# The first head drawn into TensorE's loop, and two small weights loaded ahead of the first keys, in a cached-attention decode kernel

## The chip, the cores and the metric

One core of one Trainium2 chip. The metric is device time of one execution in microseconds (us), as a median over runs. A profile's span ends some 2 us before the time, so spans are compared with spans and times with times.

## The reference, cut to what matters

```python
# x: 1 x 512; 32 heads, 65536 cached keys of 128 (bf16): K and V are 537 MB each
q = (x @ wq)                                   # 512 x 4096
scores = einsum("bhqd,bhkd->bhqk", q, k_cache) * Dh ** -0.5
o = einsum("bhqk,bhkd->bhqd", softmax(scores), v_cache)
a = o @ wo
b = (silu(x @ w_gate) * (x @ w_up)) @ w_down   # 512 x 1792, 1792 x 512
g = sigmoid((x * gate_w).sum())
return g * a + (1 - g) * b
```

Every byte of K and V is read once and used once: 1088 MB in all, with few operations for each byte.

## The kernel before

K and V pass through a ring of three slots in SBUF (the core's on-chip memory), 8.4 MB each. A head is two chunks; a chunk is one K load and one V load. VectorE multiplies K in place by q, TensorE sums the products with the identity as weights (`block`), VectorE and ScalarE finish the exponentials (`gather`), and TensorE forms P·V (`pv`). A slot is loaded again once its last reader has finished. The start shares slot 0 between wq, gate and up:

```python
dma("wq", wq_sb, ..., units(0, 0, WQ))                     # slot 0
...
load("k", 0, [EK] * (KPP // EK))                           # slot 1, four pieces
dma("gate", gate_v, ..., units(0, G0, U0))                 # slot 0
dma("up", up_v, ..., units(0, U0, U0 + KT * F))            # slot 0
load("v", 0, [KPP])                                        # slot 2
...
spread(0)                                  # q of head 0 to all partitions
for n in range(N - 1):                     # chunks, two to a head
    h, c = divmod(n, CH)
    if c == 0:
        cut[h] = len(plan.ops)
    if n:
        load("k", n, [KPP])                # the third load of the ring onwards
        load("v", n, [KPP])
    m = EK if n in (0, N - 2) else HK
    for j in range(0, KPP, m):
        ...
        block(n, j, m)
        ...
        while len(todo) > 1:
            gather()
    gather()
    if n == 0:
        gate()                             # sigmoid gate
        hidden()                           # 112 products with gate and up: frees slot 0
    ...
    pv(n)
```

All operations are recorded first and then emitted. TensorE's are emitted as straight code for head 0, a hardware loop of ten rounds of three heads (1 to 30), and straight code for head 31:

```python
first, last = 1, 1 + rounds * BODY         # BODY = 3, rounds = 10
for o in pe(0, cut[first]):
    put(o, o.waits)
...
with nc.Fori(0, rounds, 1, engines=[PE], head_slot={PE: 0}) as r:
    for i, o in enumerate(body[0]):
        put(o, {s: val + r * step[i, s] for s, val in o.waits.items()})
for o in pe(last, len(plan.ops)):
    put(o, o.waits)
```

`head_slot={PE: 0}` asks for the loop's first instruction at the start of an instruction-fetch block. TensorE's code is fetched in blocks of 16 KB, the packets of queue q8 below (13 of 16,384 bytes in the kernel before). The built program of that kernel holds 3483 entries for TensorE (instructions and 7 labels) in 222,912 bytes, 64 bytes each, so a packet holds 256.

The softmax here doesn't subtract the row's maximum and nothing guards it: scores larger than these inputs give would overflow.

## Time and profile before

| | before |
|---|---|
| median time | 2518.3 us |
| bytes moved by DMA | 1088 MB |
| mean DMA rate over the span | 432 GB/s |
| TensorE, VectorE busy | 78%, 50% |
| second K load issued; data queued before it lasts until | 52.0 us; 61.8 us |
| last V piece used by TensorE from; span | 2512.1 us; 2516.7 us |

From the page of the kernel before: the DMA row in 40 slices of the span (9 is 90% or more busy), the rate in each slice, and two of the DMA queues with packets, MB and share of 16 engines.

```profile
DMA  9999999999999999999999999999999999999998
GB/s 423 432 433 433 433 432 437 434 435 434 433 433 433 434 437 433 434 433 433 433 433 434 434 432 435 435 435 435 434 433 433 433 434 436 434 433 434 433 434 376
...
q1 hardware_dynamic: 20744, 1087.78, 99.8%
q8 instruction: 13, 0.21, 0.0%
```

The rate is flat from end to end, except for the first and last slices. The mean over the span is 432 GB/s, with most slices at 433 to 435, and the packets of q1 take 99.8% of the 16 engines' span: by that count the DMA engines are busy from end to end. (Single slices read up to 437, and windows of 78 us up to 440. The view seems to book a packet whole in one window, as 1 us windows of this run read 131 and 918 GB/s; so only means over long stretches are compared.) The page of the kernel before counts 1087.77 MB read from HBM, the chip's main memory, at 432 GB/s. So the time here is bytes over rate, plus what stands outside the stream at both ends. That no kernel could stream faster isn't shown. Queue q8 is taken as TensorE's instruction fetches: 13 packets, 0.21 MB, 16 KB each, beside 0.22 MB of TensorE code in the built program.

The chain of work that ended last tells another story at first sight. Its line by engine:

```profile
DMA 46%; PE 40%; DVE 13%; ACT 1%; issue 0%; another core or an unknown queue 0%; SPq 0%; DVEq 0%; ACTq 0%
```

It goes through TensorE and VectorE for half the span, because each load was released by them. But a load that is issued while others are still queued does not start at its issue (the second K load below is issued at 52.0 us and lands 29 us later, where its 8.4 MB take 19.3), and the chain books the queueing as "DMA". What counts is whether the queue was ever empty. That is read from the issue times. From the timeline of the kernel before, the issuing queue's loads of the start (start us, us of issuing, source):

```profile
1.03 0.38 SPq L181 DMA_DIRECT2D slot_65<-in_A_wq_dram  x1
1.47 1.96 SPq L181 DMA_DIRECT2D slot_66<-in_A_k_cache_dram  x4
3.47 0.44 SPq L181 DMA_DIRECT2D slot_65<-in_B_w_gate_dram  x1
...
4.46 0.48 SPq L181 DMA_DIRECT2D slot_67<-in_A_v_cache_dram  x1
51.99 0.33 SPq L181 DMA_DIRECT2D slot_65<-in_A_k_cache_dram  x1
52.37 0.43 SPq L181 DMA_DIRECT2D slot_66<-in_A_v_cache_dram  x1
```

And the first uses of V0 (TensorE) and of the second K load (VectorE) in the same timeline; the bracket says how long the engine had been idle and for what:

```profile
61.77 16.18 PE L257 MATMUL O_ps<-slot_67,P_sb_83 128*4 128x512 bf16 x64 [9.80 <-DMA slot_67<-in_A_v_cache_dram]
...
81.06 17.29 DVE L344 TENSOR_TENSOR slot_65<-slot_65,q_bc_78 128x16384 bf16<-128x16384 bf16 x2 [27.71 <-DMA slot_65<-in_A_k_cache_dram]
```

The second K load (slot 65) is issued at 52.0 us while V0 is still arriving until 61.8: 9.8 us of cushion. It lands at 81.06, 19.3 us after V0, which is what 8.4 MB take at 434 GB/s. VectorE's 27.7 us of idle time there cost nothing.

The tail of the kernel before, TensorE's timeline, shows two kinds of gap:

```profile
2460.93 6.10 PEld L257 LDWEIGHTS m_c<-P_sb_83,slot_65 128*128 128x128 bf16 x230 [3.16 <-issue]
2461.14 5.95 PE L257 MATMUL m_c<-P_sb_83,slot_65 128*128 128x1 bf16 x229
...
2469.42 0.86 PE L257 MATMUL m_c<-P_sb_83,slot_65 128*128 128x1 bf16 x27 [2.33 <-issue]
...
2502.09 3.44 PE L257 MATMUL m_c<-P_sb_84,slot_65 128*128 128x1 bf16 x127 [1.20 <-ACT P_sb_84 L294]
2508.09 0.18 PE L257 MATMUL m_c<-P_sb_84,slot_65 128*128 128x1 bf16 x1 [2.56 <-issue]
...
2512.12 0.77 PE L257 MATMUL m_c<-P_sb_84,slot_65 128*128 128x1 bf16 x16 [0.43 <-DMA slot_65<-in_A_v_cache_dram]
```

In the columns of P·V of the last head (a column is the 256 products that one chunk's P·V takes here), TensorE loads 128 x 128 weights at about 27 ns each. It stops twice for 2.3 and 2.6 us with no visible wait ("issue"), after 229 products of the first column and after 127 of the last. Then it waits 0.43 us for the last V piece, which ends the kernel.

### The profile page before, as it was taken

The page shows a single profiled execution, that of the slowest core. Times are in us where ns is not written, and L with a number is a line of the kernel's source. Part 1 is how long each engine was busy: PE and PEld are TensorE (multiplying, and loading weights), DVE is VectorE, ACT ScalarE, POOL GpSimd, SP SyncE. Part 2 cuts the span into 40 slices and gives each one's busy share as a digit, 9 for nine tenths or more (in the row PEclk, how much of TensorE's full clock was granted, in tenths as well). Part 3 has the DMA queues.
Part 4 walks back from the last instruction along what each step waited for, and adds up shares of the span by engine and source line. Part 5 has one row for each costly group of instructions (what it writes and reads, how often), then busy time and mean ns, then how long its engine had stood idle before and what let it go on. Part 6 is the DMA issues. An engine that isn't in the chain of part 4 may idle for free.

```text
span 2516.7 us, 15579 instructions
## 1 busy us (share of the span) xinstructions
PE 1972.7 (78%) x9177; PEld 410.3 (16%) x5215; DVE 1268.4 (50%) x291; ACT 99.2 (4%) x404; POOL 1.9 (0%) x9
## 2 busy tenths in 40 slices
PE   4777877877878778778787787787877877877787
PEld 1111111111111111111111111111111111111113
DVE  3455355464553554644545546446455364464554
ACT  0000000000000000000000000000000000000000
POOL 0000000000000000000000000000000000000000
PEclk8899989989889889899898899898988989989898
DMA  9999999999999999999999999999999999999998
GB/s 423 432 433 433 433 432 437 434 435 434 433 433 433 434 437 433 434 433 433 433 433 434 434 432 435 435 435 435 434 433 433 433 434 436 434 433 434 433 434 376
DMA packets 20767, 1088.04 MB, mean 432 GB/s; under 512 B 2314, under 2 KB 2444, under 8 KB 2700
## 3 DMA queue, kind: packets, MB, share of 16 engines
q1 hardware_dynamic: 20744, 1087.78, 99.8%
q8 instruction: 13, 0.21, 0.0%
q14 instruction: 6, 0.05, 0.0%
q10 hardware_dynamic: 4, 0.00, 0.0%
HBM read 1087.77 MB, written 0.00 MB: 432 GB/s over the span
## 4 chain that ended last, share of the span: by engine, by line
DMA 46%; PE 40%; DVE 13%; ACT 1%; issue 0%; another core or an unknown queue 0%; SPq 0%; DVEq 0%; ACTq 0%
PE O_ps L257 17%; DMA slot_67<-in_A_k_cache_dram 16%; DMA slot_65<-in_A_k_cache_dram 14%; DMA slot_66<-in_A_k_cache_dram 14%; PE S_ps_103 L275 11%; PE S_ps_104 L275 8%; DVE slot_66 L344 4%; DVE slot_67 L344 4%; DVE slot_65 L344 3%; DMA slot_65<-in_A_v_cache_dram 2%; DVE S_sb_82 L369 2%; PE m_c L257 1%; PE S_ps_103 L285 1%; ACT P_sb_83 L294 0%; DMA slot_65<-in_A_wq_dram 0%
## 5 line engine op out<-in xcount | busy, mean ns | idle before, releaser
L344 DVE TENSOR_TENSOR slot_67<-slot_67,q_bc_79 128x16384 bf16<-128x16384 bf16 (+1 forms) x28 | 208.2, 7469 | 146.5 <-DMA slot_67<-in_A_k_cache_dram 146.5
L369 DVE TENSOR_REDUCE S_sb_82<-S_ps_104 128x128 f32<-128x1024 f32 (+1 forms) x67 | 78.8, 1177 | 392.0 <-PE S_ps_104 L275 392.0
L344 DVE TENSOR_TENSOR slot_65<-slot_65,q_bc_78 128x16384 bf16<-128x16384 bf16 x22 | 190.2, 8689 | 146.3 <-DMA slot_65<-in_A_k_cache_dram 146.3
L344 DVE TENSOR_TENSOR slot_66<-slot_66,q_bc_78 128x16384 bf16<-128x16384 bf16 (+1 forms) x24 | 190.6, 7978 | 138.0 <-DMA slot_66<-in_A_k_cache_dram 122.5
L344 DVE TENSOR_TENSOR slot_66<-slot_66,q_bc_79 128x16384 bf16<-128x16384 bf16 x20 | 172.9, 8689 | 122.4 <-DMA slot_66<-in_A_k_cache_dram 122.4
L344 DVE TENSOR_TENSOR slot_65<-slot_65,q_bc_79 128x16384 bf16<-128x16384 bf16 x20 | 172.9, 8689 | 120.2 <-DMA slot_65<-in_A_k_cache_dram 120.2
L344 DVE TENSOR_TENSOR slot_67<-slot_67,q_bc_78 128x16384 bf16<-128x16384 bf16 x20 | 172.9, 8689 | 117.8 <-DMA slot_67<-in_A_k_cache_dram 117.8
L275 PE MATMUL S_ps_103<-slot_65,ident 128*128 128x512 bf16 x651 | 186.6, 457 | 0.0
L275 PE MATMUL S_ps_103<-slot_67,ident 128*128 128x512 bf16 x680 | 185.8, 441 | 0.0
L275 PE MATMUL S_ps_103<-slot_66,ident 128*128 128x512 bf16 x650 | 184.9, 454 | 0.0
L257 PE MATMUL O_ps<-slot_67,P_sb_83 128*4 128x512 bf16 x704 | 155.9, 383 | 28.1 <-ACT P_sb_83 L294 18.3
L257 PE MATMUL O_ps<-slot_66,P_sb_84 128*4 128x512 bf16 x704 | 153.7, 379 | 19.3 <-ACT P_sb_84 L294 19.3
L257 PE MATMUL O_ps<-slot_65,P_sb_83 128*4 128x512 bf16 x640 | 139.7, 379 | 18.3 <-ACT P_sb_83 L294 18.3
L257 PE MATMUL O_ps<-slot_67,P_sb_84 128*4 128x512 bf16 x640 | 139.7, 379 | 18.3 <-ACT P_sb_84 L294 18.3
L257 PE MATMUL O_ps<-slot_65,P_sb_84 128*4 128x512 bf16 x640 | 139.7, 379 | 18.3 <-ACT P_sb_84 L294 18.3
L257 PE MATMUL O_ps<-slot_66,P_sb_83 128*4 128x512 bf16 x640 | 139.8, 379 | 17.5 <-ACT P_sb_83 L294 17.5
L275 PE MATMUL S_ps_104<-slot_67,ident 128*128 128x512 bf16 x680 | 150.7, 379 | 0.0
L275 PE MATMUL S_ps_104<-slot_65,ident 128*128 128x512 bf16 x651 | 143.9, 379 | 0.0
L275 PE MATMUL S_ps_104<-slot_66,ident 128*128 128x512 bf16 x650 | 143.9, 379 | 0.0
L285 PE MATMUL S_ps_103<-slot_65,ident 128*128 128x512 bf16 x21 | 12.8, 608 | 134.9 <-DVE slot_65 L344 134.9
L285 PE MATMUL S_ps_103<-slot_66,ident 128*128 128x512 bf16 x22 | 13.2, 598 | 134.2 <-DVE slot_66 L344 134.2
L285 PE MATMUL S_ps_103<-slot_67,ident 128*128 128x512 bf16 x24 | 13.9, 581 | 125.0 <-DVE slot_67 L344 125.0
(99 smaller groups left out, 719.0 us busy)
## 6 DMA issues: line engine op xcount, KB each, us to landing
slot_66<-in_A_k_cache_dram SPq DMA_DIRECT2D x4, 2048.0 KB, 24.4
slot_67<-in_A_k_cache_dram SPq DMA_DIRECT2D x4, 2048.0 KB, 30.7
slot_65<-in_A_wq_dram SPq DMA_DIRECT2D x1, 4096.0 KB, 12.1
slot_66<-in_A_wo_dram SPq DMA_DIRECT2D x1, 4096.0 KB, 32.5
slot_65<-in_A_v_cache_dram SPq DMA_DIRECT2D x1, 4096.0 KB, 37.4
slot_65<-in_A_v_cache_dram SPq DMA_DIRECT2D x1, 2048.0 KB, 40.7
slot_65<-in_B_w_gate_dram SPq DMA_DIRECT2D x1, 1792.0 KB, 34.6
slot_65<-in_B_w_up_dram SPq DMA_DIRECT2D x1, 1792.0 KB, 38.3
```

Of the source, the lines that this page charges most:

```text
L257: ins = nc.tensor.matmul(out_ap, lhsT=a, rhs=b, start=start and i == 0, stop=stop and i == len(pairs) - 1,)
L275: ins = nc.tensor.add_instruction(mybir.InstMatmult(name=nc.get_next_instruction_name(), engine=mybir.EngineType.PE, ins=[nc.tensor.lower_ ...
L285: ins = nc.tensor.matmul(out_ap, lhsT=a, rhs=b, start=first, stop=last)
L344: "products", lambda: nc.vector.tensor_tensor(out=w, in0=w, in1=q_rep, op=ALU.mult),
L369: lambda: nc.vector.tensor_reduce(out=S_sb[b][:, :m], in_=S_ps[r][:, :m, :], axis=AXIS.X, op=ALU.add),
```

## The change

Intent: head 0 goes into the loop, so the straight code ahead of it disappears. Heads 0 to 30 are 31 = 10 x 3 + 1, so the loop runs 11 rounds and leaves the last behind the first of its three heads. For that, head 0 must look like any other head: gate and hidden layer move ahead of it, gate and up are loaded ahead of K0, K0 comes in two pieces, and a dummy O_sb feeds the diagonal that the other heads do for their predecessor.

```diff
-    load("k", 0, [EK] * (KPP // EK))
     ...
     dma("gate", ...)
     dma("up", ...)
+    load("k", 0, [HK] * (KPP // HK))
     load("v", 0, [KPP])
...
-    pending = []
+    pending = [H - 1]
...
+    gate()
+    hidden()
+
+    act("O_sb0", O_sb, ones[0:VB, 0:1].to_broadcast([VB, VB * Dh]), ACT.Copy, ["ones"], ["O_sb"])
     spread(0)
...
-        m = EK if n in (0, N - 2) else HK
+        m = EK if n == N - 2 else HK
...
-        if n == 0:
-            gate()
-            hidden()
...
-        with nc.Fori(0, rounds, 1, engines=[PE], head_slot={PE: 0}) as r:
-            for i, o in enumerate(body[0]):
-                put(o, {s: val + r * step[i, s] for s, val in o.waits.items()})
-        for o in pe(last, len(plan.ops)):
+        with nc.Fori(0, rounds + 1, 1, engines=[PE], head_slot={PE: 0}) as r:
+            turn_of(0, r)
+            with nc.tensor.If(r < rounds):
+                for i in range(1, BODY):
+                    turn_of(i, r)
+        for o in pe(cut[H - 1], len(plan.ops)):
             put(o, o.waits)
```

More of the change, by code (lines that the diff above doesn't have):

```diff
@@ L622 @@
     rounds = (H - 2) // BODY
-    first, last = 1, 1 + rounds * BODY
+    assert H == 2 + rounds * BODY
     with tc.tile_critical():
@@ L643, in pe @@
         def pe(a, b):
-            return [o for o in plan.ops[cut[a] if a else 0 : b] if o.engine == "PE"]
-        for o in pe(0, cut[first]):
+            return [o for o in plan.ops[a:b] if o.engine == "PE"]
+        for o in pe(0, cut[0]):
             put(o, o.waits)
-        body = [pe(first + r * BODY, cut[first + (r + 1) * BODY]) for r in range(rounds)]
+        heads = [pe(cut[h], cut[h + 1]) for h in range(H - 1)]
+        body = [[heads[r * BODY + i] for i in range(BODY)] for r in range(rounds)]
@@ L649 @@
+        body.append([heads[rounds * BODY]])
         step = {}
-        for i, o in enumerate(body[0]):
-            if "POOL" in o.waits:
-                nc.tensor.wait_ge(sems["POOL"], o.waits.pop("POOL"))
-            for s, val in o.waits.items():
-                step[i, s] = body[1][i].waits[s] - val if rounds > 1 else 0
-            for r, b in enumerate(body):
-                assert b[i].key == o.key, (b[i].key, o.key)
-                assert b[i].waits == {
-                    s: val + r * step[i, s] for s, val in o.waits.items()
-                }, (r, o.key, o.waits, b[i].waits)
@@ L660 @@
-        PE = mybir.EngineType.PE
-        with nc.Fori(0, rounds, 1, engines=[PE], head_slot={PE: 0}) as r:
-            for i, o in enumerate(body[0]):
-                put(o, {s: val + r * step[i, s] for s, val in o.waits.items()})
-        for o in pe(last, len(plan.ops)):
+        for i in range(BODY):
+            for j, o in enumerate(body[0][i]):
+                if "POOL" in o.waits:
+                    nc.tensor.wait_ge(sems["POOL"], o.waits.pop("POOL"))
+                for s, val in o.waits.items():
+                    step[i, j, s] = body[1][i][j].waits[s] - val
+                for r, b in enumerate(body):
+                    if i < len(b):
+                        assert b[i][j].key == o.key, (b[i][j].key, o.key)
+                        assert b[i][j].waits == {
+                            s: val + r * step[i, j, s] for s, val in o.waits.items()
+                        }, (r, o.key, o.waits, b[i][j].waits)
@@ L665, with turn_of @@
+        def turn_of(i, r):
+            for j, o in enumerate(body[0][i]):
+                put(o, {s: val + r * step[i, j, s] for s, val in o.waits.items()})
+        PE = mybir.EngineType.PE
+        with nc.Fori(0, rounds + 1, 1, engines=[PE], head_slot={PE: 0}) as r:
[4 more added lines that the diff above has]
+        for o in pe(cut[H - 1], len(plan.ops)):
             put(o, o.waits)
```

## The prediction

> **What bounds the kernel now.** The DMA engines. The page's DMA row reads 9 in every slice but the last; queue q1 holds 99.8% of 16 engines' span, and 1088 MB at a mean 432 GB/s fill the 2517 us. [...] windows of 78 us read 430 to 440. TensorE (78%) and VectorE (50%) have slack. In the DMA list a K load lands 36 us after its issue and a V load 32.5 us after, where 8.4 MB alone takes about 19.3 us at 434 GB/s: 13 to 17 us are always queued ahead. The thinnest place is the start: the second K load is issued at 52.0 us, when gate, up and the hidden layer release slot 0, and the data queued before it lasts until 61.8 us: 9.8 us of cushion. Only about 2.6 us at the front and 4.7 us at the end (last V piece landed 2512.1) are not streaming.
>
> **What the change does.**
> - Bytes: none added, none removed. WQ, gate, up, K0, V0 in place of WQ, K0, gate, up, V0; the sum is equal, so V0 should still land near 61.8 us and K1 near 81 us.
> - Gate and up land at about 21.7 us (3.67 MB take 8.5 us after WQ at 13.2). The 112 hidden products took 6.9 us, so slot 0 is free, and K1 issued, near 25 to 29 us, not 52. The cushion grows past 20 us, but nothing was starving.
> - K0's first product starts near 31.5 us instead of 18.3. After two halves of 8.7 us and their sums V1 is issued near 58 us instead of 52.4, well before K1 ends at about 81; P·V still waits for V0.
> - TensorE's straight-line code shrinks by about 390 instructions (built programs). [...] The loop body (about 1220) stays resident as before, so the new branch's target is too; no run here shows that yet. One or two fetches fewer: about 1 us of one engine's time.
> - In each round: a compare, a branch and a few register steps, well under 1 us per 232 us, hidden by TensorE's 5 to 7 us idle before each K block.
> - The extra copy into O_sb and the dummy diagonal: 0.6 and 1 us on idle engines.
>
> **On the critical path:** almost nothing. The end is set by the last V piece. TensorE has two gaps without a visible wait in the tail, 2.3 us (2467) and 2.6 us (2505.5), which I read as instruction fetches; fewer instructions shift them by 135 of 256. In the last column TensorE is only some 0.5 us ahead of the last landing, so a shift could add up to 2 us or take a few tenths off.
>
> **Predicted:** 2518.1 us, range 2516.6 to 2519.8; faster over 2%: 0.5%, within 2%: 98.5%, slower over 2%: 1%.
>
> **Right if** DMA stays near 432 GB/s in all slices, V0 lands within 1 us of 61.8, K1's issue moves to 25 to 29 us with its landing unmoved, and the spacing of heads stays 77 us. **Wrong if** the taken branch or each round's branch stalls TensorE over 13 us, draining the queue; if the slot order makes a load late; or if the last column gains a second fetch gap.

Two passages are cut from it, where marked: a ceiling for the DMA rate and a number of instructions that stay resident, which no trace or run shows, and the block size that stood beside the second. From the 2518.3 us of before the forecast takes nothing or a few tenths and comes to 2518.1. What the traces give: 256 instructions to a packet of q8, from the bytes above; and in the kernel before, q8 carries no packet from 314.2 to 2447.1 us, over nine of the loop's ten rounds, so the loop's body stays resident. That the branch's target does too is shown by the changed kernel alone (below). Of the forecast's small terms, the saved fetch was measured as one packet (13 before, 12 after, 0.9 to 1.0 us each), the copy into O_sb as 0.61 us and the dummy diagonal as 1.05 us, both in the changed kernel.

## The result, and the profile after

| | before | after |
|---|---|---|
| median time | 2518.28 us | 2518.14 us |
| lowest to highest, 4 runs each | 2518.19 to 2518.62 | 2518.11 to 2518.41 |
| span of the profiled run | 2516.7 us | 2516.4 us |
| second K load issued | 52.0 us | 29.9 us |
| second V load issued | 52.4 us | 59.1 us |
| second K load first used | 81.06 us | 81.03 us |

The ratio is 0.9999, with a 95% interval of 0.9982 to 1.0017: the same. (A ratio is the mean time of one kernel's fast runs over that of the other's fast runs of the same rounds, so it isn't quite the ratio of the medians quoted.)

The page of the changed kernel, the same lines:

```profile
DMA  9999999999999999999999999999999999999998
GB/s 423 433 433 432 434 435 433 438 433 434 433 433 433 434 435 435 435 433 433 433 433 435 434 433 432 435 436 434 435 433 433 433 433 435 434 436 433 434 433 376
...
q1 hardware_dynamic: 20456, 1087.78, 99.8%
q8 instruction: 12, 0.20, 0.0%
...
DMA 47%; PE 39%; DVE 13%; ACT 0%; issue 0%; another core or an unknown queue 0%; SPq 0%
```

The stream is as flat as before, and one instruction fetch is saved. The timeline of the changed kernel, loads of the start and first uses:

```profile
1.47 0.42 SPq L181 DMA_DIRECT2D slot_65<-in_B_w_gate_dram  x1
...
2.41 1.05 SPq L181 DMA_DIRECT2D slot_66<-in_A_k_cache_dram  x2
...
23.00 6.85 PE L285 MATMUL m_x<-Xc,slot_65 128*128 128x1 bf16 x112 [5.26 <-DMA slot_65<-in_B_w_up_dram]
29.88 0.33 SPq L181 DMA_DIRECT2D slot_65<-in_A_k_cache_dram  x1
...
59.11 0.33 SPq L181 DMA_DIRECT2D slot_66<-in_A_v_cache_dram  x1
...
61.76 13.97 PE L257 MATMUL O_ps<-slot_67,P_sb_83 128*4 128x512 bf16 x64 [2.68 <-DMA slot_67<-in_A_v_cache_dram]
81.03 17.29 DVE L344 TENSOR_TENSOR slot_65<-slot_65,q_bc_78 128x16384 bf16<-128x16384 bf16 x2 [20.69 <-DMA slot_65<-in_A_k_cache_dram]
```

The second K load is issued 22 us earlier and is used at the same instant. V0 too is used at the same instant (61.76 against 61.77). The cushion at that point grew from 9.8 us to 32, and the one at the second V load is 22 us (issued at 59.1, the K ahead of it used at 81.0). Up arrived for the hidden layer at 23.0 us. The heads follow each other every 77.28 us in both kernels (mean of 24, between VectorE's first products).

The branch records of the changed kernel, by source line (duration min/median/max in ns); L674 is the new branch, L672 the loop:

```profile
L674 PEldq COMPARE_BRANCH  x11: 77/77/208, 117.7 to 2435.7; - x11
L672 PEldq COMPARE_BRANCH  x12: 76/208/1791, 31.3 to 2436.1; - x12
```

The new branch takes 77 ns where it falls through (ten times) and 208 ns where it is taken, like the loop's own back edge (the jump to its next round). No fetch goes with them: in the changed kernel's trace q8 carries no packet from 300 to 2440 us, over nine rounds, and after the taken branch (2435.7 us) the next one starts at 2448.3. So loop and branch target stay resident. The single 1.79 us is the entry into the loop, at 31.3 us, while TensorE was waiting for VectorE until 41.5 us.

The tail, TensorE's timeline of the changed kernel:

```profile
2461.41 5.92 PE L257 MATMUL m_c<-P_sb_83,slot_65 128*128 128x1 bf16 x229
...
2469.23 0.86 PE L257 MATMUL m_c<-P_sb_83,slot_65 128*128 128x1 bf16 x27 [1.90 <-issue]
...
2502.01 3.40 PE L257 MATMUL m_c<-P_sb_84,slot_65 128*128 128x1 bf16 x127 [0.88 <-DMA slot_65<-in_A_v_cache_dram]
2507.84 0.18 PE L257 MATMUL m_c<-P_sb_84,slot_65 128*128 128x1 bf16 x1 [2.44 <-issue]
...
2511.89 0.75 PE L257 MATMUL m_c<-P_sb_84,slot_65 128*128 128x1 bf16 x16 [0.45 <-DMA slot_65<-in_A_v_cache_dram]
```

The two gaps stand after exactly the same products, 229 and 127, although some 390 instructions went from the code ahead. The prediction had them move.

### The profile page after: what moved, and what is told of

Same layout as the page of the kernel before. It is cut to its first block, busy times and chain, and to the rows that moved or that the text cites. A ratio compares the mean times of both kernels' runs of the same rounds, so it can differ in the third digit from the quotient of the medians.

```text
span 2516.4 us, 15594 instructions
## 1 busy us (share of the span) xinstructions
PE 1977.2 (79%) x9185; PEld 410.9 (16%) x5221; DVE 1268.3 (50%) x287; ACT 99.1 (4%) x402; POOL 1.9 (0%) x9
## 3 DMA queue, kind: packets, MB, share of 16 engines
q1 hardware_dynamic: 20456, 1087.78, 99.8%
## 4 chain that ended last, share of the span: by engine, by line
DMA 47%; PE 39%; DVE 13%; ACT 0%; issue 0%; another core or an unknown queue 0%; SPq 0%
PE O_ps L257 17%; DMA slot_67<-in_A_k_cache_dram 16%; DMA slot_66<-in_A_k_cache_dram 15%; DMA slot_65<-in_A_k_cache_dram 14%; PE S_ps_103 L275 11%; PE S_ps_104 L275 9%; DVE slot_67 L344 4%; DVE slot_66 L344 4%; DVE slot_65 L344 3%; DMA slot_65<-in_A_v_cache_dram 2%; PE m_c L257 2%; DVE S_sb_82 L369 2%; PE S_ps_103 L285 1%; ACT P_sb_83 L294 0%; PE S_ps_104 L285 0%
## 5 line engine op out<-in xcount | busy, mean ns | idle before, releaser
L344 DVE TENSOR_TENSOR slot_67<-slot_67,q_bc_79 128x16384 bf16<-128x16384 bf16 (+1 forms) x28 | 208.2, 7469 | 145.4 <-DMA slot_67<-in_A_k_cache_dram 145.4
L344 DVE TENSOR_TENSOR slot_65<-slot_65,q_bc_78 128x16384 bf16<-128x16384 bf16 x22 | 190.2, 8688 | 140.5 <-DMA slot_65<-in_A_k_cache_dram 140.5
L344 DVE TENSOR_TENSOR slot_66<-slot_66,q_bc_78 128x16384 bf16<-128x16384 bf16 x22 | 190.3, 8689 | 120.1 <-DMA slot_66<-in_A_k_cache_dram 120.1
L344 DVE TENSOR_TENSOR slot_65<-slot_65,q_bc_79 128x16384 bf16<-128x16384 bf16 x20 | 172.9, 8688 | 120.0 <-DMA slot_65<-in_A_k_cache_dram 120.0
L344 DVE TENSOR_TENSOR slot_66<-slot_66,q_bc_79 128x16384 bf16<-128x16384 bf16 x20 | 172.9, 8688 | 119.2 <-DMA slot_66<-in_A_k_cache_dram 119.2
L344 DVE TENSOR_TENSOR slot_67<-slot_67,q_bc_78 128x16384 bf16<-128x16384 bf16 x20 | 172.9, 8688 | 119.2 <-DMA slot_67<-in_A_k_cache_dram 119.2
L285 PE MATMUL S_ps_103<-slot_67,ident 128*128 128x512 bf16 x24 | 13.9, 579 | 125.6 <-DVE slot_67 L344 125.6
```

The lines of the kernel that those rows point to most:

```text
L285: ins = nc.tensor.matmul(out_ap, lhsT=a, rhs=b, start=first, stop=last)
L344: "products", lambda: nc.vector.tensor_tensor(out=w, in0=w, in1=q_rep, op=ALU.mult),
```

## The experiments

"Nothing changed" can be right for the wrong reason. Theory A: the transfers stream without a break, and every release of a slot has a cushion, so neither the earlier release nor the branch is felt. Rival B: two effects cancel. Rival C: TensorE's time counts and the change happens to add none. Rival D: the releases never matter at all.

### One half of the change at a time

The order alone: the loop of before, heads 1 to 30 (diff abridged).

```diff
-    load("k", 0, [EK] * (KPP // EK))         # ahead of gate and up
+    load("k", 0, [EK] * (KPP // EK))         # behind gate and up
+    gate(); hidden()                         # ahead of spread(0)
     spread(0)
-        if n == 0:
-            gate(); hidden()
```

> The load order alone: gate and up ahead of K0 and the hidden layer ahead of head 0, with the loop of before (heads 1 to 30, no branch). Theory A (the queue never emptied, so an earlier release is worth nothing): second K load issued near 30 us in place of 52, landing unmoved near 81 us, time 2518.2 +- 0.4 us. Rival B (two effects of the change cancel: the early release gains, the branchy loop loses): this run alone gains, over 0.5 us, up to the 20 us by which the release moves.

Measured: 2518.26 us (2518.12 to 2518.27, 4 runs) beside 2518.36 of before; ratio 0.9999 (0.9982 to 1.0016). The second K load is issued at 29.9 us. No gain.

The loop alone: the changed kernel with K0's load put back ahead of gate and up.

```diff
+    load("k", 0, [HK] * (KPP // HK))
     dma("gate", ...); dma("up", ...)
-    load("k", 0, [HK] * (KPP // HK))
```

> The loop alone: heads 0 to 30 in the loop with the branch, but K0 queued ahead of gate and up as before. The hidden layer still stands ahead of the loop, so TensorE waits for up near 42 us, second K load near 49 us, second V load near 76 us, still some 4 us ahead of the queue's end near 80. Theory A: 2518.2 +- 0.5 us. Rival B (cancelling effects): this run alone loses over 0.5 us. Branch records of 0.1 to 0.2 us each, as in the changed kernel.

Measured: 2519.10 us (2518.65 to 2519.72), ratio 1.0003 (0.9986 to 1.0019). All four runs lie above the median of before, by 0.3 to 1.4 us (0.7 in the median), more than the 0.5 us expected. Two of the seven runs of before in these rounds lie as high (2518.64 and 2519.01). Taken alone that speaks for B. The issue times of this run, from its timeline, name a different cause:

```profile
49.52 0.33 SPq L181 DMA_DIRECT2D slot<-in_A_k_cache_dram  x1
77.75 0.33 SPq L181 DMA_DIRECT2D slot<-in_A_v_cache_dram  x1
```

With K0 ahead of gate and up, the hidden layer waits for up, head 0's sums wait for the hidden layer, and the second V load is issued at 77.8 us, only 3.6 us before VectorE uses the K ahead of it (81.3 us in this run). The loop itself is the same as in the changed kernel, whose time is 2518.14 with the second V load at 59.1. So the loop costs nothing that shows; the 0.7 us goes with the thin cushion. How it arises there isn't shown: in the trace's packet records the DMA engines are idle for less than 0.1 us in all from 74 to 90 us, so there is no hole of that size. B needs the order alone to gain, and it doesn't. This also shows what the new load order is for: not speed, but keeping the second V load early once the hidden layer stands ahead of head 0.

### Using the cushion up

The hidden products are computed two, three or four times over (same result), which delays slot 0's release at one place:

```diff
-        group("gu", parts, ...)
+        for _ in range(4):                    # 2 and 3 in the other two
+            group("gu", parts, ...)
```

> Before with the hidden products computed twice (6.9 us more): slot 0 released near 58.9 us, still 3 us ahead of the queue's end. Theory A (cushion): no loss, 2518.3 +- 0.5 us. Rival C (start-up time on TensorE counts): +6.9 us.

> Before with the hidden products computed three times: second K load issued near 65 us. Theory A: past the threshold each us of delay costs a us; from the run with four (issue 71.5, +13.7 us) this one loses 6.5 to 7.5 us, time near 2525.3. Rival C (in proportion to the added work): +9 us; with the run of two already at +0.7 a straight line through the origin is out.

> Before, with the 112 hidden products computed four times over (20.6 us more on TensorE at one place, result unchanged): slot 0 is released at 72.6 us in place of 52.0, against data queued until 61.8. Theory A (cushion of 9.8 us): the queue runs dry once, loss of 20.6 minus 9.8 plus one to two us of issue latency, 11 to 13.5 us, time near 2530.5. Rival C (TensorE's time at the start counts in full): +20.6 us. Rival D (release of slot 0 never matters): +0.

> The changed kernel with the same 20.6 us added before slot 0's release: release near 50.5 us, second V load near 79.5, close to the end of the queued K near 80 to 81. Theory A: loss 0 to 1.5 us, time 2518 to 2519.7, against 11 to 13.5 us for the same work in before. Rival C: +20.6 us. Rival D: +0 in both kernels.

| kernel | second K load issued | time | lost |
|---|---|---|---|
| before | 52.0 us | 2518.28 us | - |
| before, twice | 58.1 | 2519.09 (2518.61 to 2520.04) | 0.8 |
| before, three times | 64.5 | 2524.98 (2524.75 to 2525.22) | 6.7 |
| before, four times | 71.5 | 2532.09 (2531.58 to 2532.20) | 13.7 |
| after, four times | 50.3 | 2520.81 (2519.72 to 2521.46) | 2.4 |

(Lost: median minus the median of before in the same rounds, 2518.26, 2518.31, 2518.36 and 2518.36 us. Issue times are of one profiled run each; that of "twice" was the slowest of its four.) From 58.1 to 64.5 us of issue (6.4 us) the loss grows by 5.8 us; from 64.5 to 71.5 (7.0 us) by 7.0. Past a threshold near 58 us each us of delay costs a us; at 52.0 nothing is lost, and no run lies between 52.0 and 58.1. The hole can be seen. Windows of before with the products four times over (the last two columns are DMA share and GB/s):

```profile
55.00:60.00 5.00, 5.00 (x86) 5.00 (x86) 0.00 (x0) 0.00 (x0) 0.00 (x0) 0.50 0.88 380
60.00:65.00 5.00, 5.00 (x87) 5.00 (x86) 0.00 (x0) 0.00 (x0) 0.00 (x0) 0.50 0.02 7
65.00:70.00 5.00, 5.00 (x87) 5.00 (x86) 0.00 (x0) 0.00 (x0) 0.00 (x0) 0.50 0.00 0
70.00:75.00 5.00, 5.00 (x34) 2.51 (x34) 0.76 (x4) 0.41 (x2) 0.00 (x0) 0.50 0.63 213
75.00:80.00 5.00, 5.00 (x19) 1.71 (x18) 0.00 (x0) 0.00 (x0) 0.00 (x0) 0.76 0.97 419
```

For 10 us almost nothing arrives. That settles against C (20.6 us expected) and D (0). The cushion that could be spent was some 6 us (71.5 minus 13.7 is 57.8, against 52.0), not the 9.8 I read off. The packet records of this run divide most of the 4 us between 57.8 and 61.8. Spread over their durations, packets fill 92% of the engines' time from 59 to 60 us, 21% from 60 to 61 and under 10% from there to 72: most of the queue ends near 60, and only a few packets of V0 land until 61.8. The first new packet starts at 72.5, 0.95 us after the issue (0.96 in the run with three). (The expectation's one to two us of issue latency was an estimate; in before, wq's first packet starts 1.0 us after its issue, and wq lands 12.1 us after it where its 4.19 MB take 9.7 at 434 GB/s.) The rest, over 1 us, stays open, and so does the 0.8 us of the run with two: its engines are idle for less than 0.1 us from 55 to 65.

The changed kernel takes the same work for 2.4 us instead of 13.7. Its delay moved to the second V load, issued at 78.4 us, 2.7 us before the use of the K ahead of it (81.06 us). I had allowed 0 to 1.5 us; the run was dearer, and has the same thin cushion as the loop alone. In both the loss lies in the stream: the last data packet lands at 2514.3 us here and 2512.2 with the loop alone, against 2511.5 in the changed kernel.

### A branch that costs something

The branch takes 0.08 to 0.2 us. To learn what it could have cost, fp32 products with no use were put in its place, in each of the 11 rounds:

```diff
             turn_of(0, r)
+            for _ in range(16):               # 32 in the second
+                nc.tensor.matmul(m_x[:, :512], lhsT=ones, rhs=ones[:, 0:1].to_broadcast([P, 512]),
+                                 start=True, stop=True)
             with nc.tensor.If(r < rounds):
```

> The changed kernel with 16 idle fp32 products[...] on TensorE at the place of the new branch, in each of the 11 rounds[...]. Theory A: TensorE waits 5 to 7 us there anyway, the rest of 7 to 9 us is under the 13 us queued ahead; loss 0 to 2 us. Rival C (TensorE's time counts): +150 us.

> The same with 32 products[...]. Theory A: 27 minus 6 of idle minus 13 of queued data, 8 us lost per round, 60 to 120 us in all. Rival C: +300 us. Rival D (never matters, TensorE has 16 us of slack in each head): +0.

(The size of one stall stood in both as an estimate that no trace gave; those passages are cut. With the measured sizes the sums come to about the same: 13.9 less 5 to 7 us of idle time leaves 7 to 9, and 27.7 less 6 and 13 leaves 8.7, where the 27 still in the second left 8; C's 150 and 300 become 153 and 305 over 11 rounds.)

Measured: with 16 (13.9 us each) 2521.99 us (2521.09 to 2523.49), 3.7 us lost over all 11 rounds; with 32 (27.7 us each) 2626.88 us (2625.4 to 2627.9), 108.6 us lost. Half the stall costs 3% of what the whole does: that is a threshold, not a rate, and both C (150 and 300) and D (0) fall. With 32 the dummy products start every 241.0 us, against 231.8 for three heads in the changed kernel: a stall in the stream costs 9.1 us, and the other 17 us or so belong to the last one, right before the tail. Windows of the run with 32 show the hole in the first round, again with DMA share and GB/s last:

```profile
150.00:155.00 5.00, 5.00 (x25) 0.00 (x0) 0.00 (x0) 0.00 (x0) 0.00 (x0) 1.00 0.97 419
155.00:160.00 5.00, 5.00 (x29) 1.16 (x10) 1.22 (x1) 0.85 (x4) 0.00 (x0) 1.00 0.15 66
160.00:165.00 5.00, 4.87 (x23) 0.00 (x0) 0.09 (x1) 0.00 (x0) 0.00 (x0) 1.00 0.00 0
165.00:170.00 5.00, 3.30 (x16) 1.34 (x17) 5.00 (x2) 0.40 (x2) 0.00 (x0) 1.00 1.10 419
```

The 3.7 us with 16 were above my 0 to 2. The chain of waits of that run ends differently from all others but that with 32:

```profile
2510.20 3.19 PE m_c L257 x128
2513.38 0.23 PE m_x L257 x2
2513.61 3.29 PE m_c L257 x128
```

No transfer is in it: in the last 80 us it is TensorE and VectorE, with under 1 us of ScalarE and some unexplained "issue". Nor is the stream late: the last data packet lands at 2511.7 us, as in before (2511.7). The stall of the last round stands right before the tail. That gave a new guess, that this one stall made the whole loss, and a run to test it, with the products inside the branch (rounds 0 to 9 only):

```diff
             with nc.tensor.If(r < rounds):
+                for _ in range(16): ...       # the same product
                 for i in range(1, BODY):
```

> The 16 dummy products (13.9 us measured) inside the branch: in rounds 0 to 9, not in the last round, right before the tail. Theory A2 (the streaming absorbs all stalls of this size; the 3.7 us of the run with 11 stalls came from the last one alone, which put TensorE behind the last landings): 2518.2 +- 0.5 us. Rival (each stall costs 0.3 us of streaming): 2521.5 us.

Measured: 2518.17 us (2517.98 to 2518.50), ratio 1.0000 (0.9983 to 1.0016). Ten stalls of 13.9 us, 139 us of TensorE's time, cost nothing at all. The 3.7 us were the last stall's: in the tail TensorE has less room than in the stream.

### Why the gaps of the tail stayed put

I had predicted that the two unexplained gaps of the tail would move by 135 instructions, because the code ahead of them shrank. They did not. Either they are no instruction fetches (rival G), or the loop's pinned head absorbs the shift (theory F): the tail starts one loop body behind a block's start in both kernels, 1244 instructions (counted in the built programs without labels, some 1220 of them products and weight loads). By the same count 1792 and 2304 instructions stand between the loop's head and the two gaps, in both kernels: 7 and 9 times 256.

```diff
-        with nc.Fori(0, rounds + 1, 1, engines=[PE], head_slot={PE: 0}) as r:
+        with nc.Fori(0, rounds + 1, 1, engines=[PE], head_slot={PE: 128}) as r:   # 64 in the second
```

> The changed kernel with the loop's first instruction placed at position 128 of a fetch block of 256 in place of 0. Theory F (the two unexplained TensorE gaps of the tail are instruction fetches, and stayed put because the loop head is pinned): both gaps come 128 instructions, 64 column products, earlier, after about 165 in place of 229 in the first column and after about 63 in place of 127 in the last. Rival G (they wait for data or a semaphore): they stay after 229 and 127. Time 2518.1 +- 1 us; more only if a second gap falls into the last column.

> The changed kernel with the loop head at position 64 of a fetch block. Theory F: first column gap after about 197 products (229 at position 0, 165 at 128). Last column: if every block boundary there can stall, gaps after about 95 and 221; the run at 128 left its second gap out, so one of them may be missing. Time 2518 to 2519.

TensorE's timeline with the head at 128:

```profile
2461.76 4.36 PE L257 MATMUL m_c<-P_sb,slot 128*128 128x1 bf16 x165
2468.13 2.56 PE L257 MATMUL m_c<-P_sb,slot 128*128 128x1 bf16 x91 [2.01 <-issue]
...
2502.20 3.34 PE L257 MATMUL m_c<-P_sb,slot 128*128 128x1 bf16 x128 [1.49 <-DMA slot<-in_A_v_cache_dram]
```

and with the head at 64:

```profile
2461.29 5.08 PE L257 MATMUL m_c<-P_sb,slot 128*128 128x1 bf16 x197
2469.50 1.71 PE L257 MATMUL m_c<-P_sb,slot 128*128 128x1 bf16 x59 [3.13 <-issue]
```

The first gap comes after 229, 197 and 165 products for a head at 0, 64 and 128: 32 products, 64 instructions, for each step of 64. F holds for it, and G falls. The fetches themselves are in the traces: a packet of q8 overlaps each of these gaps, and both gaps of the last column in before and after (in before at 2467.1 and 2505.7 us, 0.9 us each). The gap in the last column, which I had expected after 63 with the head at 128, and after 95 or 221 with it at 64, is gone in both runs (a gap of 0.26 us remains later in the column at 128); why one fetch comes with a stall and another without (in before, that at 2510.3) stays open. Times: 2518.11 us (2518.03 to 2518.32) at 128, and 2518.10 at 64 (one look). Taking 2.4 us of gap out of the last column changed nothing, since the last V piece is still used from 2511.9 us: the gap was off the critical path.

No version beats both kernels; the five best kernels here, from 2518.10 to 2518.26 us, can't be told apart.

## Why the prediction was right

The time (2518.1 predicted, 2518.14 measured): right, and so was the reason, as far as the runs can tell. That the time agrees to 0.04 us is luck: four runs of the changed kernel spread by 0.3 us.

- *The transfers bound it, at 432 GB/s.* Right: the rate is the same to 4 GB/s in every slice, and time is lost only in the runs in which a transfer hole is seen, or a load is issued within four us of the use of the one ahead, or the tail's own compute is late.
- *V0 and K1 land where they did.* Right to 0.03 us.
- *K1 issued at 25 to 29 us.* 29.9, just outside. The step that failed is the landing of gate and up, put at 21.7 us from the mean rate; the hidden layer got up at 23.0. Its own 6.9 us was right. The rate was right too: in the trace's packet records 254 of the 256 packets of gate and up have landed by 21.4 us. The last two come one after the other, at 21.9 and 22.4, while packets of K0 already land, and the first product starts 0.6 us later. The prediction had no term for such stragglers.
- *9.8 us of cushion.* Too large as something to spend: some 6 us could be spent. The term mis-sized is the queue's end, which I took from the use of V0 (61.8), when most of the DMA engines had run out near 60, and the 1 us from an issue to its first packet was left out.
- *13 us queued ahead in the stream.* Right in kind: 13.9 us of stall in ten rounds cost nothing, 27.7 us cost 9.1 us in each, so 18.6 us were absorbed, about what 13 us of queue and 5 to 7 us of idle time come to.
- *The branch costs well under 1 us and its target is resident.* Right: 77 and 208 ns. The taken branch over some 810 products and weight loads brought no fetch, and over nine rounds q8 carried no packet. How many instructions can stay resident isn't shown; the loop's 1244 did.
- *The gaps of the tail shift by 135 of 256 instructions.* Wrong. The step left out that the loop's head is pinned to a block's start, as the kernel says in `head_slot`, so here the code ahead of the loop did not move the code behind it (229 and 127 in both kernels). Moving the head moved the first gap exactly (229, 197, 165). It had no effect on the time (2518.10 and 2518.11 us).

## What to carry to other kernels

Where the transfers already stream without a hole (here 99.8% of the 16 engines' span, at 432 GB/s), ask of each change only whether some load is now issued after the queue has run dry: read each issue time against the time at which the data queued before it ends. Here a release with cushion left was worth nothing when it came earlier, and cost one for one once the cushion was spent. Test a "no effect" by spending the cushion on purpose: doubling a dose until it hurts tells a threshold from a cancellation, and a dose right before the tail must be told apart from the same dose in the stream. A small cushion was not free either: loads issued 2.7 to 3.7 us before the use of the load ahead of them cost 0.7 to 2.4 us (before with two passes, loop alone, after with four), and those issued 9.8 us or more before it cost nothing.
